# A prologue in another order, squares in scratch tiles of their own, and a last sum in two column halves

## The chip, the cores and the metric

The kernel runs on one core of a Trainium2 chip. The metric is the device time of one execution in microseconds; lower is better. Engines are named as the profile names them: PE multiplies matrices (PEld is its weight load), DVE works element by element on vectors, ACT evaluates functions and copies, POOL is a slower general engine, SP issues most transfers. Everything that PE writes goes to the accumulator memory, of which this kernel uses eight banks of 128 x 512 float32: three for a rotating buffer called mm, four for two score tiles, one for the attention output.

## The reference

One transformer-like block over a sequence of 2048 tokens of width 512, in float32:

```python
xn = layernorm(x)
q, k, v = split(xn @ wqkv)                 # 32 heads of 16
scores = q @ k.T * 16**-0.5                # causal, window of 256 keys
s = softmax(masked scores) @ v @ wo
h = silu(xn @ w1) * (xn @ w3)              # 512 -> 1792
g = silu(h @ w2)                           # 1792 -> 512
out = x + s * g
```

## The kernel before, in words

**Precision.** Every large product is made of three float16 products: each operand is cut into a high and a low half (`hi`, `lo`), and high x high, low x high and high x low are summed. Before a weight matrix can be cut it is scaled by a power of two. That power comes from the matrix itself: `squares` (line 168) sums the squares of each row, on ACT for the first `on_act` pieces and on DVE for the rest, and casts the sums; `powers` (line 196) lets PE add them up over the partitions (line 202) and DVE make the power and its inverse from the exponent (lines 204 to 209); `split` (line 216) makes `hi` on ACT and `lo` on DVE. For one group of Q and K weights these steps are called `load, norm, scale, cut` (`weights_qk`, line 267). For feed-forward weights they are `load`, `measure` and `split_pool`, which does the cut with ACT and POOL.

**Tiles.** The sequence is worked on in four tiles `t` of 512 tokens, the heads in four groups `g` of eight. For each tile `prepare` (line 303) loads four blocks of 128 tokens, makes the layer norm (`stats`, `rstd`, `centre` on DVE), and turns each block with four PE transposes (`turn`, line 335), whose result ACT casts to `XH` (line 345) and DVE subtracts to `XL` (line 350). `project` (line 394) makes Q or K of a tile and group in twelve matmuls of 512 columns, four chunks c by three terms; ACT and DVE cut the result and it is written to DRAM, from where `fetch` reads it back in another layout. `value` makes V of one block, `pass1` finds row maxima, `pass2` makes scores, exponentials and the weighted sum, `gate_up` and `down` are the feed-forward part, and `total` (line 735) multiplies by `wo`, gates, adds the residual and stores one block of 128 rows.

**Slots.** 33 slots of 2 KB a partition hold everything short-lived: raw weights, cut weights, products, scratch. `take` hands out the slot that was given back longest ago, `give` returns one. A new owner of a slot waits for the last reader or writer of the old one.

**Order.** PE's list is written by hand: it runs its instructions in the order in which the program makes them (`ORDERED`). The lists of the other engines are made by a planner, which simulates the program and takes, on each engine, the ready instruction that was made earliest; `urgent()` moves one forward, but only after the prologue. Each engine then works through its own list in order. `later(n, f)` makes f's instructions n steps later; `step` is called after each piece of matmuls, `flush` runs what is left. `spread` deals a list of matmul pieces among the batches of attention work.

**The prologue** (lines 868 to 946) loads x, the Q and K weights of groups 0 and 1, the V weights and the first feed-forward weights. Filler matmuls (`keep_busy`, line 890) occupy PE until the first blocks are centred. Then come the transposes of the four blocks into the mm banks, group 0's `scale` between them, six more fillers, group 0's `cut`, and the projections of groups 0 and 1, K before Q, with the squares, scales and cuts of the V weights and of group 1 in between. `value(0)` follows, then the first two units of attention mixed with feed-forward pieces. The squares of the fourth group (`qk[3][1]`, line 943) come after the first of these spreads and its scale three steps into the second. The program ends with four `total` calls (line 1000).

Of the kernel before, what the change touches and what calls it, by code (L numbers as in the profile page):

```python
# [19 lines left out]
P = 128  # L20
# [27 lines left out]
SLOTS = 33  # L48
# [13 lines left out]
def tile_block(ctx: ExitStack, tc: tile.TileContext, x, wqkv, wo, w1, w3, w2, out):  # L62
# [98 lines left out]
    ones = const.tile([4, KW], F16, name="ones")  # L161
# [6 lines left out]
    def squares(parts, on_act=0, apart=0):  # L168
# [4 lines left out]
        def one(i, raw):  # L173
            sq = take(BF16)
            if i < on_act:
                nc.scalar.activation(sq[:, 0:raw.shape[-1]], raw, AF.Square, accum_out=ssq[:, i:i + 1])
            else:
                nc.vector.tensor_tensor_reduce(out=sq[:, 0:raw.shape[-1]], in0=raw, in1=raw, scale=1.0, scalar=0.0,
                                               op0=ALU.mult, op1=ALU.add, accum_out=ssq[:, i:i + 1])
            give(sq)  # L180
# [35 lines left out]
    def split(hi, lo, raw, s):  # L216
        nc.scalar.activation(hi, raw, AF.Copy, scale=s)  # L217
        lasts["cut"] = nc.vector.scalar_tensor_tensor(lo, raw, s, hi, op0=ALU.mult, op1=ALU.subtract)
# [15 lines left out]
    def weights(name, w):  # L234
# [8 lines left out]
        def norm(apart=0):  # L243
            cell["sb"] = squares(cell["raw"], on_act=4 * (name == "wv"), apart=apart)
# [22 lines left out]
    def weights_qk(g):  # L267
# [11 lines left out]
        def scale():  # L279
# [3 lines left out]
            cell["sw"] = scaled(inv, WS, f"sw{g}")  # L283

            cell["es"] = es = const.tile([P, 1], F32, name=f"es{g}")
            nc.vector.tensor_scalar(es, p2, p2, DH**-0.5 / QS**2, op0=ALU.mult, op1=ALU.mult)

        def cut():
            hi = const.tile([P, 2, NC, P], F16, name=f"whi{g}")
            lo = const.tile([P, 2, NC, P], F16, name=f"wlo{g}")  # L290
            for k, raw in enumerate(cell["raw"]):
                split(hi[:, k].rearrange("p c f -> p (c f)"), lo[:, k].rearrange("p c f -> p (c f)"), raw, cell["sw"])
            give(*cell["raw"])
            WQK[g] = hi, lo, cell["es"]
# [8 lines left out]
    def prepare(t):  # L303
# [3 lines left out]
        xts = {}  # L307

        def load(b):
            xts[b] = take(F32)  # L310
            nc.sync.dma_start(xts[b], x[t * TW + b * P:t * TW + (b + 1) * P, :])
# [20 lines left out]
        def centre(b):  # L332
            nc.vector.tensor_scalar(xts[b], xts[b], mv[:, b, 0:1], rs[:, b:b + 1], op0=ALU.subtract, op1=ALU.mult)

        def turn(b):
# [4 lines left out]
            pt = psm.tile([P, NC, P], F32, name="mm", tag="mm")  # L340
# [3 lines left out]
            with urgent():  # L344
                nc.scalar.copy(xh[:, :, c], pt)
# [48 lines left out]
    def project(t, g, k):  # L394
# [3 lines left out]
        def part(half):  # L398
# [3 lines left out]
            if half == 0:  # L402
                cell["pp"] = psm.tile([P, TW], F32, name="mm", tag="mm")
            for c in (2 * half, 2 * half + 1):
                for i, (a, b) in enumerate(((hi, xh), (lo, xh), (hi, xl))):
                    nc.tensor.matmul(cell["pp"], a[:, k, c, :], b[:, c, :], start=c == 0 and i == 0,  # L406
                                     stop=c == NC - 1 and i == 2)
            if half == 0:
# [20 lines left out]
        return [(6, lambda h=h: part(h)) for h in range(2)]  # L429
# [336 lines left out]

    def feed_forward():
# [104 lines left out]
    nc.vector.memset(ones, ONE)  # L872
# [155 lines left out]
```

## Time and profile before

| | us |
|---|---|
| median of 3 runs | 888.89 (888.86 to 893.99) |
| the profiled execution | 888.72 |
| its span, from the first instruction to the last | 886.7 |
| PE busy | 851.2 (96%) |
| DVE busy | 620.3 (70%) |
| ACT busy | 442.2 (50%) |
| POOL busy | 193.9 (22%) |

The mean granted PE clock over the span is 0.993 of full. The page says where the time goes as a whole; the busy times by stage, asked for stretches of the span, say where PE is not busy; the timeline of one engine shows in brackets after a row how long the engine stood before it, and what released it. "L406" is line 406 of the program. Names of tiles stand as output<-input, without buffer numbers.

### The profile page before, as it was taken

To read this page: it belongs to the slowest core of one execution; us is meant where nothing else is said; L and a number is where in the kernel's file an instruction comes from. 1 tells how busy PE (TensorE), PEld (TensorE's weight loads), DVE (VectorE), ACT (ScalarE), POOL (GpSimd) and SP (SyncE) were. 2 spreads that over 40 slices of the span, in tenths; PEclk is the share of its full clock that TensorE was granted. 3 is DMA by queue.
4 is the path that set the end of the run, shared out by engine and by line. 5 is a ranking of instruction groups with operands and counts; after the bars stand their busy time and mean duration, and the time that the engine had idled before them with its cause. 6 is when DMAs were issued, how large, how long until landed. Compare 5 with 4: busy or idle time off the path is not lost.

```text
span 886.7 us, 20405 instructions
## 1 busy us (share of the span) xinstructions
PE 851.2 (96%) x7813; PEld 376.8 (42%) x7813; DVE 620.3 (70%) x1823; ACT 442.2 (50%) x657; POOL 193.9 (22%) x308
## 2 busy tenths in 40 slices
PE   8978998899999999999999999999999999999997
PEld 3433443444444444444444444444444444444443
DVE  6766967786767667778767776677667777676435
ACT  6776867473435444444444454444454444544521
POOL 1236236151111203111111111221111103131211
PEclk9999999999999999999999999999999999999999
DMA  9827734636643343451434334433442343422201
GB/s 289 240 85 231 225 112 128 209 109 196 167 132 84 102 125 96 131 158 52 145 102 119 106 91 131 131 102 90 136 123 59 107 133 114 116 92 85 63 11 57
DMA packets 94989, 110.51 MB, mean 125 GB/s; under 512 B 16956, under 2 KB 60076, under 8 KB 94892
## 3 DMA queue, kind: packets, MB, share of 16 engines
q1 hardware_dynamic: 94892, 109.21, 41.7%
q8 instruction: 61, 1.00, 0.5%
q14 instruction: 36, 0.29, 0.1%
HBM read 76.28 MB, written 28.57 MB: 118 GB/s over the span
## 4 chain that ended last, share of the span: by engine, by line
PE 65%; DVE 9%; issue 7%; DMA 6%; ACT 6%; SPq 4%; POOL 4%; POOLq 0%; DVEq 0%; ACTq 0%
PE mm L667 22%; PE mm L712 14%; PE po L534 8%; PE s L506 5%; PE mm L406 5%; PE mm L754 4%; PE s L459 3%; POOL slot L223 3%; DVE junk L464 3%; PE mm L380 3%; SPq L573 2%; ACT pt L524 1%; ACT slot L227 1%; DMA slot<-in_B_w_dram 1%; DMA dW<-slot 1%
## 5 line engine op out<-in xcount | busy, mean ns | idle before, releaser
L524 ACT ACTIVATE pt<-s,es 128x1024 f32<-128x1024 f32 (+1 forms) x184 | 200.8, 1093 | 233.0 <-DVE s L520 119.9
L667 PE MATMUL mm<-XH,slot 128*128 128x512 f16 x896 | 269.4, 382 | 2.1 <-DVE XL L350 1.2
L223 POOL TENSOR_TENSOR slot<-slot,slot 128x256 f16<-128x256 f32 (+1 forms) x220 | 147.4, 695 | 537.6 <-ACT slot L691 414.7
L464 DVE CUSTOM_DVE_ANT_0 junk<-s,MW 128x320 bf16<-128x320 f32 x448 | 217.8, 486 | 23.9 <-PE s L459 13.5
L667 PEld LDWEIGHTS <-slot 128*128 128x128 f16 x1344 | 122.0, 98 | 162.8 <-issue 32.2
L667 PE MATMUL mm<-XL,slot 128*128 128x512 f16 x448 | 170.8, 381 | 0.0
L712 PE MATMUL mm<-slot,slot 128*128 128x512 f16 x672 | 159.1, 380 | 0.3
L520 DVE TENSOR_TENSOR s<-s,M 128x512 f32<-128x512 f32 x128 | 89.0, 696 | 80.3 <-PE s L506 74.4
L534 PE MATMUL po<-pt,V 128*32 128x128 f32 (+1 forms) x1920 | 99.1, 333 | 0.0
L712 PEld LDWEIGHTS <-slot 128*128 128x128 f16 x672 | 60.7, 98 | 80.1 <-issue 12.9
L459 PE MATMUL s<-KA,qa 48*64 48x320 f16 (+2 forms) x1024 | 73.2, 297 | 11.4 <-DVE M L464 7.7
L506 PE MATMUL s<-qa,KA 50*64 50x128 f16 (+1 forms) x1920 | 74.2, 251 | 7.6 <-DVE M L464 4.6
L515 DVE TENSOR_TENSOR s<-s,M 128x1024 f32<-128x1024 f32 x56 | 68.8, 1228 | 17.0 <-PE s L506 14.7
L506 PEld LDWEIGHTS <-KA 50*64 50x64 f16 x1920 | 33.5, 105 | 82.3 <-issue 49.2
L682 DVE SCALAR_TENSOR_TENSOR slot<-slot,mm 128x512 f32<-128x512 f32 x56 | 38.4, 685 | 40.2 <-ACT slot L678 40.2
L691 ACT CAST slot<-slot 128x512 f16<-128x512 f32 x56 | 34.5, 616 | 54.5 <-DVE slot L687 54.5
L534 PEld LDWEIGHTS po<-pt,V 128*32 128x32 f32 x1920 | 50.2, 110 | 25.1 <-issue 12.4
L678 ACT ACTIVATE slot<-mm,sgs 128x512 f32<-128x512 f32 x56 | 38.2, 683 | 28.5 <-PE mm L667 28.2
L687 DVE SCALAR_TENSOR_TENSOR slot<-mm,slot 128x512 f32<-128x512 f32 x56 | 38.6, 689 | 18.7 <-PE mm L667 18.6
L728 DVE SCALAR_TENSOR_TENSOR slot<-mm,dsc,slot 128x512 f32<-128x512 f32 x48 | 35.9, 749 | 21.8 <-PE mm L712 21.7
L223 POOL TENSOR_TENSOR on<-on,rb 128x256 f32<-128x256 f32 x32 | 22.6, 727 | 126.5 <-DMA qa<-dm 92.5
L406 PE MATMUL mm<-XH,whi 128*128 128x512 f16 x128 | 49.2, 384 | 0.6 <-ACT whi L217 0.6
(111 smaller groups left out, 834.7 us busy)
## 6 DMA issues: line engine op xcount, KB each, us to landing
slot<-dW SPq DMA_DIRECT2D x126, 256.0 KB
slot<-in_B_w_dram SPq DMA_DIRECT2D x42, 256.0 KB
dW<-slot SPq DMA_DIRECT2D x42, 256.0 KB
slot<-in_A_x_dram SPq DMA_DIRECT2D x32, 256.0 KB
KA<-dK SPq DMA_DIRECT2D x24, 288.0 KB
qa<-dQ SPq DMA_DIRECT2D x32, 192.0 KB
dK<-slot SPq DMA_DIRECT2D x16, 256.0 KB
dQ<-slot SPq DMA_DIRECT2D x16, 256.0 KB
```

The source lines that it names most:

```text
L223: op(out[:, c], a[:, c], b[:, c])
L406: nc.tensor.matmul(cell["pp"], a[:, k, c, :], b[:, c, :], start=c == 0 and i == 0, stop=c == NC - 1 and i == 2)
L459: nc.tensor.matmul(s[64 * c:64 * c + 64, r, :n], qa[rows, 2 * p + a, ii * P + 64 * c:ii * P + 64 * c + 64], ka[rows, 2 * p + a, e - n:e], ...
L464: nc.vector.tensor_tensor_reduce(out=junk[:, :n], in0=s[:, r, :n], in1=mask, scale=1.0, scalar=NEG, op0=ALU.add, op1=ALU.max, accum_out=M[ ...
L506: nc.tensor.matmul(s[h:h + 64, r, o:o + w * P], ka[rows, 2 * p + a, (j + 2) * P + h:(j + 2) * P + h + 64], qa[rows, 2 * p + a, q * P:(q + ...
L515: nc.vector.tensor_add(sv, sv, m.unsqueeze(1).to_broadcast([P, 4, 2, P]))
L520: nc.vector.tensor_add(sv[:, :, b, :], sv[:, :, b, :], M2[:, k:k + 1, :].to_broadcast([P, 4, P]))
L524: nc.scalar.activation(pt[:, :, 0:n], s.rearrange("p r (a q) -> p (r a) q", a=2)[:, :, 0:n], AF.Exp, scale=es)
L534: nc.tensor.matmul(cell["po"][32 * i:32 * i + 32, q * P:(q + w) * P], V[:, (4 * t + j) % VB, h * VW:h * VW + 32], pt[:, i, o:o + w * P], s ...
L667: nc.tensor.matmul(cell[k], w[:, (a * NC + c) * P:(a * NC + c + 1) * P], b[:, c, :], start=c == 0 and i == 0, stop=c == NC - 1 and i == 2)
L687: nc.vector.scalar_tensor_tensor(sg, cell[1], 0.5 * HS / (WS * XS)**2, sg, op0=ALU.mult, op1=ALU.mult)
L712: nc.tensor.matmul(ps, hh[:, a * TW + b * P:a * TW + (b + 1) * P], w[:, c * D:(c + 1) * D], start=f == f0 and i == 0, stop=f == f1 - 1 and ...
```

## The change

- PE's prologue: 22 fillers instead of 40; group 0's `scale` ahead of the layer norm's `rstd`; 9 fillers; all four blocks' transposes; 4 fillers; then K and Q of group 0 term by term, side by side (four high matmuls of K, four of Q, four low-weight matmuls of each, group 1's column sums, four low-x matmuls of each). K of group 1 makes its high and low-x terms first, its low-weight term last.
- The first tile's transposes go to the scores' four banks in place of the mm banks.
- Half of the first tile's x loads are issued by ACT.
- Group cuts make K's half (k = 1) before Q's, and the scale factor `es` after the cut. `issue_after(i)` puts what is made in its block behind instruction i on i's engine: the K half's `lo` after the last centring, the Q half's `hi` after the last `XH`, the last two `XL` after the last `lo`; group 1's and the V weights' squares after `hi` on ACT and after `XL` on DVE, and so on.
- Squares write their elementwise result to four scratch tiles (two for ACT, two for DVE) instead of slots; slots fall from 33 to 32; the row of ones for the keys sits in a slot for a while. V's squares are half on ACT (2 of 4), the first feed-forward squares 4 of 6.
- The fourth group's squares are made at the sixth step of the first spread.
- The last block's `total` is made in two halves of 256 columns, each with its own twelve matmuls, two DVE operations and store.

```diff
-SLOTS = 33
+SLOTS = 32
...
         def one(i, raw):
-            sq = take(BF16)
+            sq = ppool.tile([P, D], BF16, name="sqa" if i < on_act else "sqd", bufs=2)
...
     def split(hi, lo, raw, s):
-        nc.scalar.activation(hi, raw, AF.Copy, scale=s)
+        lasts["hi"] = nc.scalar.activation(hi, raw, AF.Copy, scale=s)
...
-            cell["sb"] = squares(cell["raw"], on_act=4 * (name == "wv"), apart=apart)
+            cell["sb"] = squares(cell["raw"], on_act=2 * (name == "wv"), apart=apart)
...
-            nc.sync.dma_start(xts[b], x[t * TW + b * P:t * TW + (b + 1) * P, :])
+            (nc.scalar if t == 0 and b % 2 else nc.sync).dma_start(xts[b], x[t * TW + b * P:t * TW + (b + 1) * P, :])
...
-            pt = psm.tile([P, NC, P], F32, name="mm", tag="mm")
+            if t:
+                pt = psm.tile([P, NC, P], F32, name="mm", tag="mm")
+            else:
+
+                if b % 2 == 0:
+                    pair["s"] = pss.tile([P, 2, 512], F32, name="s")
+                pt = pair["s"][:, b % 2, :].rearrange("p (k q) -> p k q", q=P)
...
-    def project(t, g, k):
+    def project(t, g, k, terms=(range(3),)):
...
+        parts = ([[(c, i) for c in (2 * half, 2 * half + 1) for i in range(3)] for half in range(2)] if len(terms) == 1
+                 else [[(c, i) for i in group for c in range(NC)] for group in terms])
...
-        sb = squares([raws[0][0], raws[1][0], raws[0][1], raws[1][1], RAW[f][1], RAW[f + 1][1]], on_act=6 if f == 0 else 4, apart=apart)
+        sb = squares([raws[0][0], raws[1][0], raws[0][1], raws[1][1], RAW[f][1], RAW[f + 1][1]], on_act=4, apart=apart)
...
+    def total_by_columns(t, b):
...
+        for c in (slice(0, 256), slice(256, 512)):
+            ps = psm.tile([P, 256], F32, name="mm", tag="mm")
+            for g in range(NG):
+                for i, (a, w) in enumerate(((0, WOH), (0, WOL), (1, WOH))):
+                    nc.tensor.matmul(ps, O[t, g][:, a, tb], w[:, g, c], start=g == 0 and i == 0,
+                                     stop=g == NG - 1 and i == 2)
+            nc.vector.scalar_tensor_tensor(y[:, c], ps, sc["y"], y[:, c], op0=ALU.mult, op1=ALU.mult)
+            nc.vector.tensor_add(y[:, c], y[:, c], xr[:, c])
+            nc.sync.dma_start(out[r, c], y[:, c])
...
-    keep_busy(40)
+    keep_busy(22)
     for b in range(4):
         stats0(b)
     qk[0][1]()
+    qk[0][2]()
+    keep_busy(9)
     rstd0(0, 4)
     for b in range(4):
         centre0(b)
-    qk[1][1]()
+    with tc.issue_after(lasts["centre"].ins):
+        qk[0][3]((1,))
     for b in range(2):
         turn0(b)
-        step()
-    qk[0][2]()
+    step()
     for b in range(2, 4):
         turn0(b)
-        step()
-    keep_busy(6)
-    flush()
-    qk[0][3]()
-
-    k00 = project(0, 0, 1)
-    run(k00[:1])
-    wv[1]()
+    with tc.issue_after(lasts["xh"].ins):
+        qk[0][3]((0,))
+    with tc.issue_after(lasts["cut"].ins):
+        flush()
+    with tc.issue_after(lasts["hi"].ins), tc.issue_after(lasts["x"].ins):
+        qk[1][1]()
+        wv[1]()
+    keep_busy(4)
+
+
+    k00, q00 = (project(0, 0, k, ((0,), (1,), (2,))) for k in (1, 0))
+    run([k00[0], q00[0], k00[1], q00[1]])
     qk[1][2]()
-    run(k00[1:])
-    with tc.issue_after(lasts["cut"].ins):
-        qk[1][3]()
-    run(project(0, 0, 0))
+    qk[1][3]()
+    with tc.issue_after(lasts["hi"].ins):
+        run([k00[2], q00[2]])
+    later(1, lambda: fetch(0, 0))
+    k01 = project(0, 1, 1, ((0, 2), (1,)))
+    run(k01[:1])
     wv[2]()
-    later(1, lambda: fetch(0, 0))
-    run(project(0, 1, 1))
-    with tc.issue_after(lasts["cut"].ins):
+    with tc.issue_after(lasts["hi"].ins), tc.issue_after(lasts["cut"].ins):
         wv[3]()
-        sc["uv"] = scaled(SQ["wv"][2], 1.0 / (WS * XS), "uv")
-        sc["o"] = scaled(SQ["wv"][3], OS, "so")
+    run(k01[1:])
+    sc["uv"] = scaled(SQ["wv"][2], 1.0 / (WS * XS), "uv")
+    sc["o"] = scaled(SQ["wv"][3], OS, "so")
+    with tc.issue_after(lasts["hi"].ins):
         measure(0)
...
     started.append(True)
+    later(6, qk[3][1])
     spread(batches(None, units[0]), value(2) + value(3) + more(EARLY // 2))
-    qk[3][1]()
     later(3, qk[3][2])
...
-        run(total(NT - 1, b))
+        if b < 3:
+            run(total(NT - 1, b))
+    total_by_columns(NT - 1, 3)
     flush()
```

More of the change, by code (lines that the diff above doesn't have):

```diff
@@ L428, in part @@
             later(1, rest)
-        return [(6, lambda h=h: part(h)) for h in range(2)]
+        return [(len(l), lambda n=n: part(n)) for n, l in enumerate(parts)]
     def fetch(t, g):
@@ L871, in tile_block @@
     wout = weights("wo", wo)
-    nc.vector.memset(ones, ONE)
+    ones = take(F16)
+    nc.vector.memset(ones[0:4, 0:KW], ONE)
     for b in range(4):
@@ L934, in tile_block @@
         for q in range(2):
[L935 removed]
+            nc.sync.dma_start(KA[r][64 * q + KR:64 * q + KR + 2], ones[2 * q:2 * q + 2, 0:KW].unsqueeze(1).to_broadcast([2, 4, KW]))
+    give(ones)
     qk[2][1]()
```

59 lines of the change are left out of this document (36 added, 23 removed).

## The prediction

> **What bounds the kernel now.** I read the page first, then the busy times by stage, then PE's timeline where a stage is thin, and from there the engine that PE waited for.
>
> The page's first part (busy us, share of the span, instructions), and from the busy times by stage (us; then PE, PEld, DVE, ACT, POOL busy with counts; PEclk; DMA share; GB/s):
>
> ```profile
> PE 851.2 (96%) x7813; PEld 376.8 (42%) x7813; DVE 620.3 (70%) x1823; ACT 442.2 (50%) x657; POOL 193.9 (22%) x308
> ...
> 0.00:18.10 18.10, 15.23 (x64) 6.94 (x64) 12.72 (x44) 10.84 (x26) 3.39 (x24) 1.00 0.97 285
> 140.00:870.00 730.00, 716.48 (x6904) 318.01 (x6902) 513.77 (x1444) 340.54 (x458) 140.01 (x209) 1.00 0.39 113
> ```
>
> PE is the bound: 716 of 730 us in the long middle, at full clock. So a microsecond that PE's list starts earlier is a microsecond of the span, unless something else then makes PE wait. The change touches only the thin places, the start and the end, so it is worth what PE idles there and no more. In the first stage PE's 15.23 us are mostly the filler of line 893. PE's own timeline there (start, us, what; in brackets the idle time and its releaser):
>
> ```profile
> 1.06 11.70 PE L893 MATMUL ps<-onesb 128*128 128x512 bf16 x40 [1.06 <-DVE onesb L136]
> 12.59 1.04 PE L342 MATMUL mm<-identf,slot 128*128 128x128 f32 x8
> 15.57 0.63 PE L342 MATMUL mm<-identf,slot 128*128 128x128 f32 x4 [1.00 <-DVE XL L350]
> 16.08 1.47 PE L893 MATMUL ps<-onesb 128*128 128x512 bf16 x6
> 18.11 0.39 PE L406 MATMUL mm<-XH,whi 128*128 128x512 f16 x1 [0.56 <-ACT whi L217]
> 18.95 0.39 PE L406 MATMUL mm<-XH,wlo 128*128 128x512 f16 x1 [0.45 <-DVE wlo L218]
> ...
> 29.25 0.38 PE L380 MATMUL mm<-wvh,XH 128*128 128x512 f16 x1
> ```
>
> The first projection matmul runs alone at 18.11, and the stream begins at 18.95. From there 47 more projection matmuls reach 29.25 without a wait, (29.25 - 18.95)/47 = 0.219 us each with the small matmuls between. An unbroken stream of 48 would have started at 18.73. That is the number to beat.
>
> The second thin place, with ACT's rows around it and the busy times by stage:
>
> ```profile
> 51.09 0.72 ACT L226 ACTIVATE slot<-slot,pi 128x512 f32<-128x512 f32 x1 [2.15 <-DVE pi L618]
> 57.28 0.63 ACT L176 ACTIVATE slot<-slot 128x512 bf16<-128x512 f32 x1
> 58.88 0.19 PE L202 MATMUL ps<-sb,onesb 128*128 128x1 bf16 x2 [5.13 <-DVE sb L189]
> 64.53 0.57 ACT L415 ACTIVATE slot<-mm 128x512 f16<-128x512 f32 x1
> ...
> 53.40:58.90 5.50, 0.37 (x3) 0.09 (x2) 0.86 (x2) 5.50 (x13) 4.72 (x8) 0.93 0.22 72
> 58.90:61.60 2.70, 2.70 (x12) 0.76 (x11) 1.60 (x8) 2.48 (x5) 0.00 (x0) 0.51 0.00 0
> 71.80:75.20 3.40, 1.37 (x18) 0.55 (x17) 2.50 (x10) 1.29 (x4) 1.30 (x2) 1.00 0.92 237
> 75.20:78.60 3.40, 3.40 (x10) 1.16 (x9) 3.06 (x14) 2.52 (x5) 1.30 (x2) 0.50 1.05 393
> ```
>
> PE stands 5.13 us for the column sums of the fourth group's weights. Their squares (57.28) come last in a run of ACT that is busy 5.50 of 5.50 us with the cuts of feed-forward weights. Then the granted clock is 0.51 for 2.70 us, which is half of that, 1.3 us, lost. This is the largest single stall of the trace.
>
> **The change part by part. The start.** The rows that make up today's 18.73, on DVE, ACT and SP's queue, and the row of the squares that DVE makes:
>
> ```profile
> 10.54 1.00 DVE L333 TENSOR_SCALAR slot<-slot,mv,rs 128x512 f32<-128x512 f32 x2
> 11.46 0.17 DVE L189 CAST sb<-ssq 128x2 bf16<-128x2 f32 x1
> 11.53 1.00 DVE L333 TENSOR_SCALAR slot<-slot,mv,rs 128x512 f32<-128x512 f32 x2
> 13.70 0.16 DVE L204 TENSOR_SCALAR al<-ps 128x1 f32<-128x1 f32 x1 [1.09 <-PE ps L202]
> 13.90 0.15 DVE L206 TENSOR_SCALAR al<-al 128x1 int32<-128x1 int32 x1
> 17.48 0.75 DVE L218 SCALAR_TENSOR_TENSOR wlo<-slot,sw,whi 128x512 f16<-128x512 f32 x1
> ...
> 8.70 0.63 ACT L176 ACTIVATE slot<-slot 128x512 bf16<-128x512 f32 x1 [0.18 <-DMA slot<-in_A_wqkv_dram]
> 14.14 1.54 ACT L345 CAST XH<-mm 128x512 f16<-128x512 f32 x3
> 16.24 0.58 ACT L345 CAST XH<-mm 128x512 f16<-128x512 f32 x1
> 16.72 1.33 ACT L217 ACTIVATE whi<-slot,sw 128x512 f16<-128x512 f32 x2
> ...
> 0.74 1.80 SPq L311 DMA_DIRECT2D slot<-in_A_x_dram  x4
> ...
> L178 DVE CUSTOM_DVE_ANT_0 slot<-slot x16: 675/686/1139, 24.0 to 238.6; 128x512 bf16<-128x512 f32 x16
> ```
>
> The first two centred blocks stand at 11.54, but PE is in its filler until 12.76, and the fourth block's transposes wait for a bank until 15.57. The change cuts the filler to 22 + 9, puts all four blocks into the scores' four banks, moves the squares of all other weights off ACT until the casts are through, and scales group 0 before the blocks are centred. New order, counted: the group's cast and five scale operations at 0.2 us each (13.70 to 13.90 is one step) now lie among DVE's centring, so the last block is centred at 12.53 + 1.2 = 13.7 at worst and 12.5 at best. Its four transposes take 1.04/8 x 4 = 0.5. ACT has four casts (1.54/3 = 0.5 each, 0.58 alone) and one weight half (1.33/2 = 0.67) to do from about 12: 12 + 4 x 0.55 + 0.67 = 14.9, and cannot end before the last transposes at 13.1 plus 0.58, 13.7. I take **14.5** for the first projection matmul, 4.2 earlier than 18.73. Bounds: 13.7, and 16.4 if the column sums stay behind the second centring as the cast at 11.46 does today (PE then makes them at 11.7, its nine fillers end at 13.7, sixteen transposes take 2.1, and the last cast 0.58).
>
> The two x loads on ACT's queue save two issues of 1.80/4 = 0.45 on SP; at 285 GB/s and a DMA share of 0.97 no more than that 0.9 can come of it, and since ACT's square at 8.70 waits for data I count nothing. On ACT they stand ahead of nothing before 7 us.
>
> What the new order adds: by terms (high x high, low, x low) the K and Q projections of group 0 run side by side, and group 1's column sums stand in PE's list after sixteen matmuls, 16 x 0.219 = 3.5 us after 14.5, at 18.0. Behind them stand all of PE's later work. Its two squares on ACT (0.63 each) may start when the last weight half is out, 15.2, and are done at 16.5; the cast must wait on DVE for all four x-low subtractions and may come behind two squares of value weights (line 178): 17.5 to 18.9. So a wait between 0 and 0.9 us there, and the same again for group 1's halves. I take 0.9 in all, up to 2. Group 0's low half (0.75 on DVE) is covered by the eight high matmuls (1.7 us) that now precede it. The start is worth 4.2 - 0.9 = **3.3** (bounds 0.3 to 5.0).
>
> **The fourth group's squares.** Issued at the sixth step of the first spread, they come while ACT idles: before 51.09 stands an idle stretch of 2.15 us, and the two squares take 1.3. PE's 5.13 and the 1.3 at half clock go: **6.4**. Next late is ACT itself: the read at 64.53 of the last projection's bank lies behind the same cuts, and without the squares (2 x 0.63) they end only 1.3 us earlier, where PE would like it 6.4 earlier. The planner orders that read anew, so I charge a fraction, **1.3**, and keep 0 and 6.4 - 1.3 = 5.1 as ends.
>
> **The last sum.** PE's end and what follows it, two DVE rows of one operation at 320 and 128 columns for the slope, and the group of the last sums' weight loads (busy us, mean ns of one):
>
> ```profile
> 881.76 0.38 PE L754 MATMUL mm<-woh,O 128*128 128x512 f16 x1
> 882.17 0.75 DVE L758 SCALAR_TENSOR_TENSOR slot<-mm,us,slot 128x512 f32<-128x512 f32 x1 [1.11 <-PE mm L754]
> 882.96 0.69 DVE L760 TENSOR_TENSOR slot<-slot,slot 128x512 f32<-128x512 f32 x1
> ...
> 50.26 0.48 DVE L464 CUSTOM_DVE_ANT_0 junk<-s,MW 128x320 bf16<-128x320 f32 x1
> 51.52 0.28 DVE L464 CUSTOM_DVE_ANT_0 junk<-s,M 128x128 bf16<-128x128 f32 x1
> ...
> L754 PEld LDWEIGHTS <-O 128*128 128x128 f16 x48 | 4.5, 98 | 6.8 <-ACT O L578 1.0 <-POOL O L223 0.6
> ```
>
> (0.48 - 0.28)/192 is 1.04 ns a column, so 256 columns fewer save 0.27 in each of two operations: 0.5. The last store has half the bytes, 128 KB or 0.4 us at 285 GB/s. Against that stand 24 matmuls of half width for 12: a weight load takes 0.098, a half-width matmul should take 0.219/2 = 0.11, so the twelve loads more are hidden, or at the worst add 12 x 0.098 = 1.2. It is nearest to hidden, and I take off 0.2. **0.7**, bounds -0.3 and 0.9.
>
> At nothing I cost: scratch for squares in tiles of its own (it takes a pretended owner out of the slots); two of the value weights' and two of the first feed-forward squares on DVE instead of ACT (0.69 each, counted above where they could be late); the ones in a slot (set at the start, read by DMAs after the projections).
>
> **Sum**: 3.3 + 6.4 - 1.3 + 0.7 = 9.1. The profiled execution took 888.72 (its span 886.7 and 2.0 around it), 0.17 below the median, so 879.6 there and **879.8** as a median.
>
> **A rule weighed.** After 53.40:58.90, with 0.37 of PE work, comes half clock; after 71.80:75.20, with 1.37 of 3.40, comes it too. In the start, 12.59 to 18.11 holds 1.47 us of filler beside the transposes, and the clock stayed at 1.00. The Trainium skill, "TensorE: Matmul & The Clock Gate", Part 1, says half rate follows an idle window of about 3.4 us and lasts one window, and Part 4 that transposes don't count as busy. The trace agrees on the length (75.20 to 78.60) but not that the window must be idle. By the two parts together the new start, with 13 fillers around its transposes, could fall to half clock; the sum by that is 881.5 (rival 1 prices it), by today's row 879.8.
>
> **Rivals.**
> 1. *The clock drops in the new start.* The 22 fillers end 18 x 0.219 = 3.9 us before today's 12.76, at 8.8. From there to 14.5 PE has 13 more, 2.8 us, the transposes, and waits. Half of 3.40 is 1.7 lost: 881.5. Against it: the row of today's start, with less filler, at 1.00. Chance 0.10, within 1%.
> 2. *ACT takes the stall's time back*, with the full 5.1: 888.9 - 3.3 - 6.4 + 5.1 - 0.7 = 883.6. For it the 5.50 of 5.50; against it ACT's 2.15 idle and that the first matmuls behind the stall read nothing that ACT makes after 58.88. 0.10, within 1%.
> 3. *The squares move in the program and not on ACT*, whose order the planner makes: the stall stays, 888.9 - 3.3 - 0.7 = 884.9. 0.07, within 1%.
> 4. *Slower: one slot fewer.* From the chain of waits, and line 672's own row (duration ns, first and last start us; two of these stores belong to a block of feed-forward columns):
>
> ```profile
> 73.78 6.24 DMA dW<-slot
> 80.03 0.61 ACT slot L227
> ...
> L672 SPq DMA_DIRECT2D dW<-slot x28: 319/424/1315, 38.9 to 209.8; - x28
> ```
>
> A cut waits 6.24 us for its slot to be written out. The 14 blocks of the first tile follow each other at (209.8 - 38.9)/13.5 = 12.7 us and take eight slots each (three raw, three cut, two for their products): one every 1.6 us. With 32 slots every reuse comes a turn sooner; where the slot is the last wait, PE loses 1.6 a block, 14 x 1.6 = 22 in all, and 888.9 - 9.1 + 22 = 902. It is over 1% slower once the wait binds at twelve blocks. Against: one such wait in the chain, and squares no longer take slots out of turn. 0.08.
> 5. *More than forecast*: nothing given back (10.4 + 0.9), and the half clock at 75.20 goes too, 1.7: 888.9 - 13.0 = 876. 0.15.
>
> **How the numbers follow.** The forecast has 0.50, and the bounds of its parts give 877 to 883; 1% of 888.9, about what a measurement here can tell from no change, is at 880.0, so I split it 0.30 to 0.20. Faster: 0.30 + 0.15 = 0.45; within 1%: 0.20 + 0.10 + 0.10 + 0.07 = 0.47; slower 0.08. The range runs from 875, a little under case 5, to 887, case 3 with ACT giving back another 2; it leaves out case 4 and the far ends.
>
> **What would show it.** Right: PE's first L406 near 14.5, value's first matmul near 26, no PE wait over 1 us on the fourth group's column sums, PEclk 1.00 after it, a last store after two DVE operations of about 0.45. Wrong: column sums of group 0 or 1 waiting over 1 us for their cast, ACT's read of the last projection as PE's new releaser, PEclk at 0.5 before 20 us, or long DMA waits on slots between 60 and 200 us.

## The result, and the profile after

| | before | after |
|---|---|---|
| median of 20 runs each, us | 889.20 (887.12 to 893.99) | 886.48 (883.94 to 889.44) |
| after / before, 95% interval | | 0.9969 (0.9956 to 0.9981) |
| the profiled execution, us | 888.72 | 888.54 |
| its span, us | 886.7 | 886.8 |

The change makes the kernel 2.7 us faster (1.7 to 3.9). The forecast was 9.1. The profiled execution of after lies 2.1 above the median of its runs, that of before 0.5 below, so the two spans agree by chance, and what is compared below are places within the spans. PE's own timeline of the changed kernel (start, us, what; in brackets the idle time and its releaser):

```profile
14.37 0.66 PE L353 MATMUL s<-identf,slot 128*128 128x128 f32 x4 [0.73 <-ACT XH L356]
15.72 1.89 PE L421 MATMUL mm<-XH,whi 128*128 128x512 f16 x8
...
22.35 1.04 PE L421 MATMUL mm<-XH,whi 128*128 128x512 f16 x4 [1.24 <-ACT whi L215]
...
27.95 0.38 PE L391 MATMUL mm<-wvh,XH 128*128 128x512 f16 x1
...
31.30 0.17 PE L200 MATMUL ps<-sb,onesb 128*128 128x6 bf16 x1 [0.60 <-DVE sb L187]
31.73 0.38 PE L391 MATMUL mm<-wvh,XH 128*128 128x512 f16 x1 [0.26 <-DVE al L202]
...
38.66 0.41 PE L474 MATMUL s<-KA,qa 48*64 48x256 f16 x8
...
52.45 0.17 PE L200 MATMUL ps<-sb,onesb 128*128 128x6 bf16 x1 [5.32 <-DVE sb L187]
...
60.15 0.19 PE L200 MATMUL ps<-sb,onesb 128*128 128x1 bf16 x2
...
882.73 0.27 PE L796 MATMUL mm<-woh,O 128*128 128x256 f16 x1
```

The start first. The stream of projections begins at 15.72 instead of 18.73, 3 us earlier. It then waits 1.24 us for group 1's high half, and V's first matmul, at 29.25 before, stands at 27.95: 1.3 us are left. Two waits of 0.60 and 0.26 follow on the first feed-forward sums. The eight score matmuls at 38.66 stand in the trace of before so:

```profile
38.81 0.41 PE L459 MATMUL s<-KA,qa 48*64 48x256 f16 x8
```

The lead there is 0.15 us. The new start has given back nearly all that it won by the time it ends.

Even that lead is an accident of the one execution of before. Six traces of this study hold the old start. The row stands at 38.13 to 38.17 in three of them (e3, e4, e12 of the experiments), at 38.59 in e6, at 38.70 in e9, and latest, at 38.81, in before. Five traces hold the new start without half clock in it (after, e1, e2, e5, e10): 38.66 to 38.84. In before the 40 fillers end late. The busy times of the first stretch, before's and then e12's, and e12's row:

```profile
0.00:6.94 6.94, 5.88 (x14) 2.04 (x15) 3.64 (x10) 1.28 (x1) 3.39 (x24) 1.00 0.70 218
0.00:6.94 6.94, 5.89 (x21) 2.41 (x22) 4.40 (x12) 1.28 (x1) 3.39 (x24) 1.00 0.76 220
38.15 0.41 PE L457 MATMUL s<-KA,qa 48*64 48x256 f16 x8
```

In 5.88 us before makes 14 fillers, e12 21. Until 6.94 us those of before start 0.43 us apart, later ones 0.22, so PE begins at half speed for a time that differs between executions, though the row's PEclk reads 1.00. So the start that the prediction set out to beat was itself late: V's first matmul comes at 28.60 in e12 and at 29.25 in before.

The second thin place has not become thick, it has moved. The fourth group's column sums, which stood 5.13 us at 58.88 before, come at 60.15 without a wait. But 8 us ahead of them the *feed-forward* column sums (six columns, not one) now wait 5.32 us. The timelines of ACT, DVE and SP's queue in the same trace, and then the busy times of two stretches (us; PE, PEld, DVE, ACT, POOL busy with counts; PEclk; DMA share; GB/s):

```profile
47.89 0.62 ACT L706 CAST slot<-slot 128x512 f16<-128x512 f32 x1 [2.63 <-DVE slot L702]
48.41 0.63 ACT L175 ACTIVATE sqa<-slot 128x512 bf16<-128x512 f32 x1
...
53.32 0.61 ACT L175 ACTIVATE sqa<-slot 128x512 bf16<-128x512 f32 x1
...
49.78 0.47 DVE L187 CAST sb<-ssq 128x2 bf16<-128x2 f32 x1 [0.70 <-ACT sqa L175]
52.22 0.17 DVE L187 CAST sb<-ssq 128x6 bf16<-128x6 f32 x1 [1.97 <-ACT sqa L175]
...
35.64 2.64 SPq L980 DMA_DIRECT2D KA<-slot  x4
38.38 0.95 SPq L271 DMA_DIRECT2D slot<-in_A_wqkv_dram  x2
```

```profile
49.24:52.45 3.21, 0.00 (x0) 0.00 (x0) 0.65 (x2) 3.21 (x11) 0.98 (x2) 0.50 0.94 277
52.45:56.07 3.62, 3.62 (x16) 1.23 (x16) 3.35 (x19) 2.74 (x8) 0.00 (x0) 0.50 0.03 8
```

From 48.41 to 53.84 ACT makes nine squares one behind another. The first two are the fourth group's: the cast of two columns follows them at 49.78. The next four are the feed-forward's: the cast of six columns follows at 52.22, and PE, idle from 47.13, gets its sums at 52.45. Half clock (PEclk 0.50) covers 49.24 to 56.07, of which 3.62 us fall on work. ACT had idled 2.63 us just before all this. None of the nine squares waits for its data in the trace; they stand where the planner put them, behind the cast at 47.89. The fourth group's weights were only asked for at 38.38, behind the rows of ones for the keys (line 980).

### The profile page after: what moved, and what is told of

It reads as the page before. It is cut to its first block, busy times and chain, and to the rows that moved or that the text cites. A ratio compares the mean times of both kernels' runs of the same rounds, so it can differ in the third digit from the quotient of the medians.

```text
span 886.8 us, 20443 instructions
## 1 busy us (share of the span) xinstructions
PE 847.0 (96%) x7814; PEld 375.9 (42%) x7814; DVE 623.7 (70%) x1833; ACT 441.1 (50%) x649; POOL 193.4 (22%) x308
## 4 chain that ended last, share of the span: by engine, by line
PE 70%; DVE 9%; ACT 6%; DMA 5%; issue 5%; POOL 3%; SPq 1%; POOLq 0%; DVEq 0%; ACTq 0%
PE mm L682 25%; PE mm L727 14%; PE po L549 8%; PE mm L421 6%; PE s L521 6%; PE s L474 4%; PE mm L769 4%; PE mm L391 3%; DVE junk L479 3%; POOL slot L221 2%; DMA slot<-in_A_x_dram 1%; ACT pt L539 1%; DMA slot<-in_B_w_dram 1%; ACT sqa L175 1%; ACT slot L225 1%
## 5 line engine op out<-in xcount | busy, mean ns | idle before, releaser
L421 PE MATMUL mm<-XH,whi 128*128 128x512 f16 x128 | 47.1, 381 | 1.2 <-ACT whi L215 1.2
```

## The experiments

Every time is a median, the ratio that of the kernel's runs to runs of before on the same chip, with its 95% interval. "after" and "before" are the two kernels of the change.

**The fourth group's squares.** Three kernels move nothing but them.

e1, after, with the squares back behind the spread:

```diff
-    later(6, qk[3][1])
     spread(batches(None, units[0]), ...)
+    qk[3][1]()
```

> The changed kernel with one part undone: the fourth group's squares back behind the first spread. My theory (the move traded one stall for another): the column sums of the third and fourth feed-forward block no longer wait (5.32 us in the changed kernel), the fourth group's own sums wait about 5.1 us again as before the change, and the time is that of the changed kernel within 2 us. If the move is worth most of the 6.4 us of my forecast and the start is what failed, this kernel is 4 to 6 us slower than the changed one. If the scratch tiles alone hold up the feed-forward squares, their wait of about 5 us stays here and the two stalls add up: 5 us slower.

Measured: 885.67 us, 0.9941 (0.9922 to 0.9959), 5.0 under before where after is 2.7 under it. PE's timeline of e1:

```profile
48.48 0.17 PE L200 MATMUL ps<-sb,onesb 128*128 128x6 bf16 x1
...
59.95 0.19 PE L200 MATMUL ps<-sb,onesb 128*128 128x1 bf16 x2 [5.12 <-DVE sb L187]
```

The feed-forward sums no longer wait, and the old stall is back at its old size. So the move traded one stall for the other, and rather lost by it. Up to 870 us the trace of e1 has 3.41 us of half clock, that of after 10.24 (one execution each).

e2, after, with the squares at the ninth step (`later(9, qk[3][1])`):

> The changed kernel with the fourth group's squares made at the ninth step of the first spread instead of the sixth, so that they are made behind the feed-forward squares of the same spread. My theory: both stalls are gone, ACT runs two of the feed-forward squares about 10 us earlier and the fourth group's squares before the cuts; no wait over 1 us for column sums between 40 and 62 us; 4 to 6 us faster than the changed kernel, 880.5 to 882.5. Rival, ACT's work is the bound here (the cuts are only moved to where PE waits for them next): within 2 us of the changed kernel, with a new wait of 3 us or more between 55 and 80 us. Rival, the loads of the fourth group's weights are what is late: the wait on its own column sums comes back with about 5 us.

Measured: 887.58 us, 0.9964 (0.9947 to 0.9980), no better than after. The theory missed. ACT's timeline has the feed-forward squares well ahead, the last at 42.13, but DVE and PE show why that does not help:

```profile
52.98 0.24 DVE L187 CAST sb<-ssq 128x2 bf16<-128x2 f32 x2 [1.92 <-ACT sqa L175]
...
53.27 0.18 PE L200 MATMUL ps<-sb,onesb 128*128 128x6 bf16 x1 [2.95 <-DVE sb L187]
```

On DVE's list the cast of the fourth group's two columns stands ahead of the cast of the six, so the sums that are ready wait for the squares that are not.

e3, before, with the squares at the sixth step and nothing else changed:

```diff
     started.append(True)
+    later(6, qk[3][1])
     spread(batches(None, units[0]), ...)
-    qk[3][1]()
```

> The kernel before with nothing but the fourth group's squares made at the sixth step of the first spread (the squares still write to slots, 33 of them). My theory: the stall of 5.13 us on the fourth group's sums goes, a stall of about 4 to 6 us on the feed-forward blocks' sums comes in its place, and the time is that of the kernel before within 2 us. Rival, the new scratch tiles or the slot fewer make the new stall: no wait over 1 us here, and 5 to 6.4 us faster than before.

Measured: 893.81 us, 1.0042 (1.0025 to 1.0059), 3.1 us slower. PE's timeline:

```profile
51.73 0.17 PE L202 MATMUL ps<-sb,onesb 128*128 128x6 bf16 x1 [5.33 <-DVE sb L189]
...
59.45 0.19 PE L202 MATMUL ps<-sb,onesb 128*128 128x1 bf16 x2
```

The same stall in the same place without scratch tiles and without the new start: the move alone makes it.

e5, after, with the load of the fourth group ahead of the rows of ones. The one line is all:

```diff
+    qk[3][0]()
     for r in range(3):
...
     qk[2][3]()
-    qk[3][0]()
```

> The changed kernel with one statement moved: the load of the fourth group's weights is made ahead of the six writes of the keys' row of ones and ahead of the second half of V's first products, so that on SP's queue it stands ahead of them and of the dK and dQ transfers instead of behind (issue at 38.6 us before). My theory: the late load is the common cause of both stalls; with the data there early, ACT makes the fourth group's squares and all four feed-forward squares in its idle time before 47 us, neither column sum waits over 1 us between 40 and 62 us, and the kernel is 4 to 6.5 us faster than the changed one. Rival, the cuts on ACT take the time back (ACT is the bound of this stretch): a new wait of 3 us or more on something that ACT makes between 55 and 80 us, within 2 us of the changed kernel. Rival, earlier loads delay the dK and dQ transfers behind them: the first attention matmuls move from 34.5 us by over 1 us.

Measured: 881.65 us, 0.9902 (0.9876 to 0.9928), 9.0 under before, 6.3 more than after. SP's queue, ACT and PE in the trace of e5:

```profile
19.50 1.06 SPq L271 DMA_DIRECT2D slot<-in_A_wqkv_dram  x2
...
40.18 0.64 ACT L175 ACTIVATE sqa<-slot 128x512 bf16<-128x512 f32 x1
...
43.81 0.64 ACT L175 ACTIVATE sqa<-slot 128x512 bf16<-128x512 f32 x1
...
54.81 0.19 PE L200 MATMUL ps<-sb,onesb 128*128 128x1 bf16 x2
74.95 0.25 PE L474 MATMUL s<-KA,qa 48*64 48x128 f16 x4 [2.33 <-ACT pt L539]
```

The load goes out at 19.50 instead of 38.38. ACT has all six squares done by 44.45, where it had idled before, and neither column sum waits. The 6.3 us hold the move's own loss too. What the move is worth with an early load is read against e1, which leaves the squares behind the spread: 9.0 - 5.0 = 4.0 us by the medians (their intervals just touch) and 5.1 by the two traces at 870 us. The forecast of this part was 5.1. The next wait is a new one, 2.33 us at 74.95, on an exponential that stands on ACT behind feed-forward cuts.

**The scratch tiles.** The prediction priced them at nothing. e6 is before with e3's and e5's edits: early load, early squares, results still in slots.

> The kernel before with two statements moved and nothing else: the fourth group's load ahead of the keys' rows of ones, its squares at the sixth step of the first spread. My theory: the stall of 5.13 us goes and none comes for it: 5 to 6.4 us faster than before, about 884.5, as my forecast had it for this part alone. Rival, the time is given back on ACT: 1 to 3 us faster.

Measured: 890.15 us, 0.9986 (0.9971 to 1.0001): nothing. The theory missed. PE and DVE of e6:

```profile
78.04 0.25 PE L459 MATMUL s<-KA,qa 48*64 48x128 f16 x4 [3.47 <-ACT pt L524]
...
78.11 1.14 DVE L178 CUSTOM_DVE_ANT_0 slot<-slot 128x512 bf16<-128x512 f32 x1 [4.54 <-POOL slot L223]
```

Matched one to one, the matmuls of e6 lead those of before by 6.5 us just ahead of the wait at 78.04, and by 0.3 at 84.74: what was won at 59 us is lost there. The last row names a resource that the prediction did not price: a DVE square whose elementwise result nobody reads stands 4.54 us for the slot it is to be thrown into, which POOL still uses. Two kernels put that to the test, one from each side. e9 is e6 with scratch tiles (and 32 slots, the ones in a slot), but the old start and the old last sum; e10 is e5 with the results back in slots (and 33 of them):

```diff
-            sq = take(BF16)
+            sq = ppool.tile([P, D], BF16, name="sqa" if i < on_act else "sqd", bufs=2)
...
-            give(sq)
```

> As e6_before_load_and_squares (the kernel before, the fourth group's load and squares earlier), and the squares' results go to four scratch tiles with 32 slots, as in the changed kernel; the start and the last sum stay as before. In e6 the 5.67 us won at 59 us were gone at 112 us: the column sums of the next feed-forward blocks waited 2.19 us at 67.9 us and a score tile 3.47 us at 78 us for ACT, and a square on DVE stood 4.54 us for a slot that POOL still used. If the slots of the squares are what gives the time back, those waits go and this kernel is 4 us or more faster than before. Rival, the new start is what e5 has and e6 has not: as e6, within 1.5 us of before.

> As e5_load_earlier, but the squares' results go to slots again, 33 of them. If the slots of the squares are what gives the time back, the waits of e6 between 65 and 85 us come back and it is 4 us or more slower than e5. Rival, the scratch tiles cost and bring nothing (as my forecast counted them): within 1.5 us of e5.

Measured: e9 881.26 us, 0.9894 (0.9876 to 0.9912), 9.4 under before where e6 was 0.5 under it. e10 888.57 us, 0.9972 (0.9957 to 0.9986), 2.1 under before where e5 was 9.0. The rows of DVE's squares in the grouped view of e9 and then e10 (busy us, mean ns of one; idle time before them and what ended it):

```profile
L177 DVE CUSTOM_DVE_ANT_0 sqd<-slot 128x512 bf16<-128x512 f32 x16 | 11.8, 749 | 4.8 <-DMA slot<-in_B_w_dram 4.8
```

```profile
L177 DVE CUSTOM_DVE_ANT_0 slot<-slot 128x512 bf16<-128x512 f32 x20 | 15.0, 766 | 7.3 <-POOL slot L222 7.1 <-DMA dW<-slot 0.2
```

In slots, DVE stands 7.1 us for POOL; in tiles of their own, only for the weights themselves. PE's wait of 78.04 does not go with it, though. The same exponential holds PE in e9:

```profile
76.09 0.25 PE L457 MATMUL s<-KA,qa 48*64 48x128 f16 x4 [3.88 <-ACT pt L522]
```

At last e12, before with scratch tiles, 32 slots and the ones in a slot, everything else as it was:

> The kernel before with the squares' results in four scratch tiles, 32 slots and the row of ones in a slot, and nothing else. The 5.13 us stall of the fourth group stays. My theory (the scratch tiles are the working part of the change): DVE's squares no longer wait for slots that POOL uses (5.0 us of idle time ahead of them before), and it is 3 to 4.5 us faster than before. Rival, they only let other gains through and bring nothing alone: within 1 us of before. Rival, one slot fewer costs: slower.

Measured: 884.22 us, 0.9929 (0.9910 to 0.9949), 6.0 us faster (4.5 to 8.0), more than the theory and both rivals gave. The part priced at nothing is the largest of the change, and larger than the whole change. The same edit brings 8.9 us from e6 to e9, and without the ones, which both have in a slot, 6.9 from e10 to e5. So that it works is shown three times. How it works is not what the theory said. The rows of DVE's squares in before and in e12:

```profile
L178 DVE CUSTOM_DVE_ANT_0 slot<-slot 128x512 bf16<-128x512 f32 x16 | 11.4, 715 | 5.0 <-POOL slot L223 5.0
```

```profile
L177 DVE CUSTOM_DVE_ANT_0 sqd<-slot 128x512 bf16<-128x512 f32 x16 | 11.8, 744 | 7.7 <-DMA slot<-in_B_w_dram 7.7
```

The 5.0 us for POOL are gone, but 7.7 us for the weights have come, so DVE's squares stand longer than before. Where the time is won can be read by matching matmuls: the two kernels of a pair run the same PE list, and the lead is the difference between the starts of the same matmul. For e12, e4 stands in for before (the same program up to its last block; its fillers end nearly when e12's do):

| start of the matmul in e4 or e6, us | 40 | 70 | 240 | 560 | 590 | 860 |
|---|---|---|---|---|---|---|
| lead of e12 over e4, us | 0.0 | 0.8 | 2.3 | 4.2 | 5.7 | 5.8 |
| lead of e9 over e6, us | -0.1 | 1.5 | 6.0 | 7.2 | 8.8 | 8.6 |

The last square of any of these kernels stands before 240 us. In e12 more than half of the gain comes after it, and in both pairs some 1.5 us come between 560 and 590. There DVE's list is in another order. DVE and PE of before, and then PE of e12:

```profile
568.27 1.03 DVE L749 SCALAR_TENSOR_TENSOR slot<-slot,slot 128x512 f32<-128x512 f32 x1
571.03 0.33 PE L459 MATMUL s<-KA,qa 48*64 48x320 f16 x4 [0.85 <-DVE M L464]
```

```profile
567.87 0.33 PE L457 MATMUL s<-KA,qa 48*64 48x320 f16 x4 [0.22 <-DVE M L462]
```

In before a step of a `total` stands ahead of the row maxima for which PE waits, in e12 behind them. So a part of what the scratch edit brings comes from the planner's new order of DVE's work, far from any square. Before and e4, one program up to the last block, are themselves 2.1 us apart at 860 us, so the leads show where the time is won and not to the tenth how much.

**The new start.** e13 is before with the new start alone (results in slots, 33 slots, the fourth group's squares and the last sum as they were):

> The kernel before with the new start alone: order of PE and DVE, transposes in the score banks, x loads on two queues, V's squares half on ACT, feed-forward squares four on ACT; squares' results in slots (33), the fourth group's squares behind the first spread, the last sum whole. My forecast had 3.3 us for it. My theory now: its waits of its own use it up, and it is within 1 us of before. Rival, it is what e1 has: 3 to 4.5 us faster.

Measured: 889.47 us, 0.9991 (0.9972 to 1.0009), that is 0.7 us, from 2.5 faster to 0.8 slower. It agrees with e5 and e9, which differ by the start and the last sum and stand at 9.0 and 9.4 under before. Two kernels look for what holds the start up. e8 is e5 with the transposes of the four blocks in four different tiles (one mm, both score tiles, the attention output's), where after pairs two blocks in one score tile:

```diff
-                if b % 2 == 0:
-                    pair["s"] = pss.tile([P, 2, 512], F32, name="s")
-                pt = pair["s"][:, b % 2, :]...
+                if b == 0:
+                    pt = psm.tile([P, NC, P], F32, name="mm", tag="mm")
+                elif b < 3:
+                    pt = pss.tile([P, 2, 512], F32, name="s")[:, 0, :]...
+                else:
+                    pt = pso.tile([P, TW], F32, name="po")...
```

> As e5_load_earlier, and the four blocks' transposes go to four tiles (an mm bank, one bank of each score tile, the attention output's bank) instead of pairs in two tiles. My theory: the second and the fourth block's transposes no longer wait for the cast of the block before in the same tile (0.68 and 0.73 us); the first projection matmul moves from 15.8 to 14.5 to 15 us. Whether the time follows depends on group 1's scale, which DVE sets: I expect the wait at 22.5 us to grow by what is won, so within 0.7 us of e5. Rival, the order of PE is the bound there: 1.2 us faster than e5.

Measured: 880.51 us, 0.9887 (0.9868 to 0.9905), 1.5 thousandths under e5 and inside both intervals. PE's timeline:

```profile
14.11 1.89 PE L424 MATMUL mm<-XH,whi 128*128 128x512 f16 x8
20.76 1.04 PE L424 MATMUL mm<-XH,whi 128*128 128x512 f16 x4 [1.26 <-ACT whi L215]
```

The first projection comes 1.6 us earlier than after's 15.72, so the shared tile was what held the transposes (their waits in after were 0.68 and 0.73). The wait for group 1's half is untouched, where the theory had it grow. The 1.65 us that e8 leads e5 by still stand at 39 us; at 70 us, behind a wait of 2.60 on feed-forward sums, e8 is 3.9 us late. e7 goes at the wait for group 1's half: e5, with V's squares on DVE put behind group 1's scale factor, which had to queue after them and the feed-forward's:

```diff
-        nc.vector.tensor_scalar(t, a, by, None, op0=ALU.mult)
+        lasts["sw"] = nc.vector.tensor_scalar(t, a, by, None, op0=ALU.mult)
...
-        wv[1]()
...
+    with tc.issue_after(lasts["sw"].ins):
+        wv[1]()
```

> As e5_load_earlier, and V's two squares on DVE are held behind group 1's scale factor on DVE. My theory of the start (its gain is eaten by its own new waits): the wait of 1.24 us for group 1's first weight half at 22.5 us goes or falls under 0.3 us, value's first matmul moves from 28.1 to under 27.2 us, and the time falls by up to 1 us against e5. Rival, the wait only moves (V's own sums come later by as much): value's first matmul stays at 28 us and the time with it.

Measured: 878.63 us, 0.9861 (0.9839 to 0.9883), 12.0 under before and the best of all. The wait of 1.24 is gone (PE's timeline):

```profile
21.26 1.04 PE L421 MATMUL mm<-XH,whi 128*128 128x512 f16 x4
...
74.43 0.25 PE L474 MATMUL s<-KA,qa 48*64 48x128 f16 x4 [2.61 <-ACT pt L539]
```

That is 3.0 us under e5 on the same chip, more than the wait of 1.24, but the intervals overlap and the two profiled executions are 0.7 apart. Their traces don't show the start as the reason: new waits of 0.56 and 0.41 come for the one that went, the wait on the feed-forward sums grows from 0.61 to 1.13, e7 is 0.5 us behind e5 at 39 us and level with it at 80. A part may be the clock: the mean granted clock of e7's runs is 0.9978, that of e5's 0.9942, and 0.0036 x 880 = 3.2 us at most. e11 puts both mends together, loads the fourth group still earlier, ahead of V's stage, and holds the first feed-forward squares on DVE behind V's scale factor (beside the edits of e7 and e8):

```diff
-    with tc.issue_after(lasts["hi"].ins):
+    with tc.issue_after(lasts["sw"].ins):
         measure(0)
+    qk[3][0]()
     run(project(0, 1, 0))
...
-    qk[3][0]()
     for r in range(3):
```

> The changed kernel with all that the runs so far point to: the fourth group's load ahead of the second projection's Q half, V's squares on DVE behind group 1's scale factor, the transposes in four tiles, and the first feed-forward squares free on ACT (behind V's scale factor on DVE). If the waits at the start add up and are all mended: value's first matmul near 25.5 us, no wait of 0.6 us for the first feed-forward sums, and 1 to 2 us faster than e7 (878.6), about 877. Rival, something that the start does not set holds the kernel at 84 us, where e5 and e7 stood at the same time: as e7 within 1 us.

Measured: 881.78 us, 0.9908 (0.9887 to 0.9929), no better than e5. The theory missed and the rival held. PE's timeline:

```profile
67.16 0.17 PE L200 MATMUL ps<-sb,onesb 128*128 128x6 bf16 x1 [2.60 <-DVE sb L187]
74.89 0.25 PE L477 MATMUL s<-KA,qa 48*64 48x128 f16 x4 [2.82 <-ACT pt L542]
```

Whatever the start wins meets ACT at 74 to 75 us: the same exponential holds PE at 74.95 in e5, 74.43 in e7 and 74.89 here. At 60 us e11 leads e5 by 3.3 us, at 77 it is 1.2 behind.

**The last sum.** e4, before with the last block's `total` in column halves:

> The kernel before with nothing but the last block's sum in two halves of columns. By the two profiles (4.92 us from the start of the last matmul to the end before, 4.03 after) 0.9 us faster than before, by my forecast 0.7; if the twelve more weight loads cost what they take alone, 0.3 slower. Either way within 1 us of before.

Measured: 890.26 us, 0.9991 (0.9973 to 1.0008), 0.4 us, not to be told from nothing. The two traces agree with the forecast all the same: from the start of PE's last matmul to the end of the span are 4.92 us before (886.68 - 881.76) and 4.03 after (886.76 - 882.73). DVE's two last operations and the group of weight loads, in after:

```profile
883.04 0.48 DVE L798 SCALAR_TENSOR_TENSOR slot<-mm,us,slot 128x256 f32<-128x256 f32 x1 [0.29 <-PE mm L796]
883.56 0.42 DVE L799 TENSOR_TENSOR slot<-slot,slot 128x256 f32<-128x256 f32 x1
```

```profile
L796 PEld LDWEIGHTS <-O 128*128 128x128 f16 x24 | 2.4, 98 | 0.5
```

The operations took 0.75 and 0.69 before. The twelve loads more cost no idle time worth naming.

## Why the prediction was wrong

| part | forecast, us | measured, us | read from |
|---|---|---|---|
| start | 3.3 (0.3 to 5.0) | 0.7 (-0.8 to 2.5) | e13 |
| fourth group's squares | 5.1 (1.3 to 6.4) | -3.1 (-5.3 to -2.2) | e3 |
| the same with an early load | | 4.0 (3.4; in slots 0.5) | e5 against e1 (e9 against e12; e6) |
| last sum | 0.7 (-0.3 to 0.9) | 0.4 (-0.7 to 2.4) | e4 |
| scratch, 32 slots | 0 | 6.0 (4.5 to 8.0) | e12 |

The measured parts of the change add to 0.7 - 3.1 + 0.4 + 6.0 = 4.0, where the whole gave 2.7 (1.7 to 3.9).

**"The fourth group's squares ... come while ACT idles": this step failed, in sign.** ACT does idle before 51.09, as the row said, and idles in after too. But the step costed the squares alone, not the load that they read, which the change leaves where it was, in SP's queue behind the six writes of the rows of ones; with the load early (e5) the planner puts the squares at 40.18 instead of 48.41. And it asked where the squares go, not what stands behind them: made earlier than the next feed-forward squares, they come ahead of them on ACT, their cast comes ahead on DVE, and each engine works through its list in order. PE's 5.13 us went and 5.32 came. The half clock did not go either. What the step expected comes true in e5, with one line moved. Rival 3, squares that move in the program but not on ACT, came nearest in time (884.9) and had the wrong mechanism: they did move. The e1 and e3 comparisons put the move at a loss of 2.3 and 3.1 us; e1's and after's intervals just touch, e3's excludes zero.

**"At nothing I cost: scratch for squares in tiles of its own": this step failed, and it hid the other.** A reason was given, that it takes a pretended owner out of the slots, and no price, though DVE's squares in slots stood 5.0 us for POOL in the profile of before. That row is no price either: the waits went, others came, and a part of the gain lies where no square is made. So 0 against 6.0 is shown, and how much of it is the slots and how much the planner's new order stays open. Without the 6.0 us of this part the others add to 2.0 us slower than before. It also decides whether gains elsewhere are kept: the early load and squares bring 0.5 us in slots (e6) and 3.4 us on top of scratch (e9 against e12, intervals that just touch).

**The start was mis-sized: 3.3 stands against 0.7.** The first projection comes at 15.72, not 14.5. The prediction let the transposes run as fast as the blocks were centred; two blocks that share a score tile wait for each other's casts, 0.68 and 0.73 us (e8 takes that out: 14.11). The new waits, charged at 0.9 with up to 2 as their end, came to 2.1: 1.24 us on group 1's half, where it was named, and 0.86 on the first feed-forward sums, where none was. With the stream 1.2 us later than assumed and 2.1 us of waits, 0.9 of the 4.2 should be left at 32 us; the row at 38.66 has 0.15. V's first matmul came at 27.95, not "near 26". And the 18.73 to beat was read from the latest of the old starts: over the traces counted above the row at 38 us stands no earlier in the new one.

**The last sum was right** in its mechanism and, by the two traces, in its size (0.9 for 0.7); no run can confirm a time so small.

**The rivals.** Rival 1, half clock in the new start, did not happen in the profiled execution of after. It did in that of e13, the same start (below), so it happens in some executions. The price of 1.7 was too low there: e13's first projection comes at 19.02, 3.3 us behind after's 15.72. Rival 2, ACT takes the time back, is seen one stage further on: the exponential behind the cuts at 74 to 75 us. Rival 4, one slot fewer, is refuted: e12 has 32 slots and is 6.0 us faster.

**The rule weighed.** The prediction went by one row, today's start at full clock. That row was one execution. The last section shows the old start at half clock too.

**The sum.** "877 to 883" does not follow from the parts: their low ends, 0.3 + 6.4 - 5.1 - 0.3 = 1.3, give 887.6.

**Open**: how much of the 6.0 us of e12 is the slots and how much the planner's new order, which a kernel with scratch tiles and the old lists would tell; and why e7's runs are faster than e5's, beside the clock.

## What to carry to other kernels

A dead result needs an owner too: ask whose buffer it lands in and who still uses that buffer, since a square here stood 4.54 us for a place whose content nobody reads. A change of buffers also lets a planner order the whole program anew, so its price isn't read from one wait. A step that is moved is only as early as its load in the transfer queue, and once on an in-order list it delays what was there before it, on every engine that it touches. A term that looks like nothing deserves its row as much as one that looks large.

## What was not expected of the hardware

The granted clock changes on a grid of 3.413 us: within each trace all edges of the half-clock stretches lie whole multiples of that apart (in before 58.14 - 6.94 = 15 x 3.413), but the grid lies differently against the program in each execution. The busy times of three kernels, cut along their grids: e12 around the old stall at 59 us, e9 in the old start, e13 in the new one:

```profile
51.74:55.15 3.41, 0.83 (x4) 0.29 (x3) 1.16 (x4) 3.41 (x7) 2.91 (x5) 1.00 0.00 0
55.15:58.57 3.42, 0.87 (x5) 0.32 (x5) 0.71 (x5) 3.42 (x8) 2.23 (x4) 0.50 0.35 117
58.57:61.98 3.41, 3.41 (x16) 1.01 (x15) 2.62 (x9) 3.19 (x8) 0.00 (x0) 0.50 0.00 0
```

```profile
11.56:14.97 3.41, 1.66 (x15) 1.32 (x14) 2.06 (x10) 3.20 (x9) 0.00 (x0) 1.00 1.15 311
14.97:18.38 3.41, 3.38 (x10) 1.76 (x11) 2.78 (x6) 3.01 (x8) 0.00 (x0) 0.50 1.16 311
```

```profile
7.44:10.85 3.41, 1.39 (x9) 0.68 (x9) 3.07 (x21) 1.00 (x4) 0.00 (x0) 1.00 1.10 347
10.85:21.09 10.24, 8.89 (x29) 4.87 (x28) 5.71 (x13) 6.01 (x14) 0.00 (x0) 0.50 1.15 313
```

A stretch at full clock with little PE work is followed by one at half. Cut so, without the last 25 us of each, the fifteen traces of this study hold 30 stretches at full clock in which PE was busy 1.48 us or less; 28 were followed by half clock. Of eight with 1.61 to 1.67 us seven were, of 19 with 1.7 to 2.0 two, and none above. Of 45 stretches at half clock, nine had PE busy for 2.74 us or less, and eight of these were followed by another; none of the rest was. So the same stall brings one stretch of half clock or two by where the grid falls: around the old stall of 5.13 us before has 3.41 us of it in its profiled execution, e12 6.83. In e13 half clock lies over three stretches of the new start, and its first projection comes at 19.02. This may be part of why single executions of one kernel differ by several us (after: 883.94 to 889.44), and a forecast of a stall's price then holds for a median at best.

The Trainium skill, "TensorE: Matmul & The Clock Gate", Part 1, gives a free-running window of 3413 ns. The traces agree on both. It says that half rate follows an idle window; here it followed windows in which PE was busy for up to 1.99 of 3.41 us (e5, from 128.28), and the measurement decides.
